# Float32 second products for block 1 of stage 1 and block 0 of stage 2, their weights split later, weight bits further ahead, idle products at the start

## The chip, the cores and the metric

One core of a Trainium2 chip runs the whole program. The metric is device microseconds of one execution; before the change the median of three runs is 1176.47 us (1175.05 to 1176.57). The core has five engines with their own in-order queues: PE (matrix products into PSUM; PEld is its weight load), DVE (elementwise), ACT (activation functions and copies), POOL (elementwise, and issue of its own DMAs) and SP, which here only issues DMAs.

## What is computed

Three things follow each other for 6080 tokens of 256 channels: a gated recurrence, a feed-forward with a rational activation, and a feed-forward with a squared relu. Both feed-forwards have 2048 hidden channels.

```python
f = lb + (1 - lb) * sigmoid(f_logit);  i = 1 - f
h[t] = f[t] * h[t-1] + i[t] * x[t]                  # over t; the recurrence's output is x1

h  = x1 @ w_in                                      # stage 1
P  = a0 + a1*h + a2*h**2 + a3*h**3
Q  = 1 + |b0|*|h| + |b1|*h**2
x2 = (P / (Q + 1e-6)) @ w_out

r  = maximum(x2 @ moe2_w_in, 0)                     # stage 2
out = (r * r) @ moe2_w_out
```

The weights arrive as 64-bit floats, two 32-bit words each.

## The kernel before

**Tiling.** The tokens are cut into 12 blocks (`BLOCKS`, one of 448, then eleven of 512). The hidden channels are cut into `NP` = 8 chunks of 256; a chunk's tile is 128 partitions x 2 x tokens. For block j and chunk i each stage does a first product into PSUM (`S1_mm1` into `h`, `S2_mm1` into `hb`), an elementwise chain, and a second product that adds to the block's accumulator over the eight chunks (`S1_mm2`, `S2_mm2` into `acc`). I call step s = 8j + i the turn in which chunk i of block j goes through stage 1. Stage 2 of the same block and chunk follows `LAG` = 9 steps later, so steps 0 to 7 are block 0 of stage 1 alone, steps 8 to 15 are block 1 (with block 0 of stage 2 from step 9 on), and so forth.

**Two kinds of product.** A product of float32 precision is made in one of two ways (`mm1`, `mm2`, lines 317 to 340). Either both operands stand as one float32 tile each, then there are 4 float32 matmuls to a group; or each operand stands as a high and a low part in the format fp32r, and three terms (high x high, low x high, high x low) are added, 12 matmuls that each run faster. In the trace one float32 matmul shows as two records. Block 0 of stage 1 is made with float32 products; all else with three terms.

**The chain of stage 1** (lines 381 to 445). ACT makes `u` = |h| (L387) and the linear part `s` (L394), from block 1 on POOL makes `t` from `u` (L389; in block 0 ACT squares h and PE adds the quadratic `q` with two diagonal matrices, L414). DVE makes the polynomial (L400, L401) and, from block 1 on, the quadratic (L408); ACT the reciprocal (L422, L423); DVE the ratio (L427, L430) and L441. The result goes to the second product as `g` in block 0 (L558), or as a high part on ACT (`s1_high`, L436) and a low part on DVE (`s1_low`, L444). In stage 2 ACT makes relu (L451), the square (L458) and the high part (L459), POOL the low part `g2l` one step later (`s2_low`, L464). When `acc` of a block is complete, ACT and DVE split it into `x2h` and `x2l` (L472, L473).

**Weights.** There are 32 chunks of weights, named by matrix and number: i1, o1 (stage 1, first and second product) and i2, o2. Each is loaded by SP (`load`), scaled by ACT (`scale`, L164), turned into float32 by three instructions on DVE (`bits`, L169, L178, L181, into a tile called `wa` or `whole`), and then split (`split_w`: two copies on ACT, L190 and L191, and one accumulating DMA from POOL's queue, L192). A float32 product uses the tile before its split.

**What sets the order.** The order is written out by hand, and each engine executes its own instructions in that order. One loop (lines 567 to 608) writes steps 0 to 7, a second (610 to 682) all the others. `h` has one buffer in PSUM (two in block 0), so the next first product waits until the polynomial has read it. In steps 8 to 16 the second loop makes bits and splits of i2 and o2 chunk by chunk, with these lines among others:

```python
wi = index["i2", s - NP] if s - NP < NP else None
wo = index["o2", s - LAG] if 0 <= s - LAG < NP else None
```

At the start the tokens of block 0 are turned by PE transposes (L225), gated and scanned; `first_gate`, `first_mul`, `pre_scan` come before the first `S1_mm1` (line 564), with the bits of chunk i1,0. The tokens of later blocks are prepared one block ahead (`ahead`: transposes, multiplications and scans on DVE, tanh on ACT, in steps 3 to 6 of a block).

## Time and profile before

| what | value |
|---|---|
| median of the runs | 1176.47 us |
| the profiled execution | 1175.87 us |
| its span, first to last instruction | 1174.1 us |
| PE busy | 1111.7 us (95%) |
| DVE busy | 986.9 us (84%) |
| ACT busy | 910.8 us (78%) |
| POOL busy | 416.3 us (35%) |

Busy shares over the whole span hide that the kernel has stretches with different limits. The span cut in 40 equal slices shows PE at 5 to 9 tenths in the first eight and at 9 in nearly all that follow, and DVE the other way at 9 in most of the first eight. The rows of a timeline give the start, the duration, the engine with its line, what is written and read with its shape, and in brackets how long the engine was idle before it and what ended that. Consecutive instructions of an engine overlap a little, so I take the distance from start to start as what one costs.

### The profile page before, as it was taken

To read this page: it belongs to the slowest core of one execution; us is meant where nothing else is said; L and a number is where in the kernel's file an instruction comes from. 1 tells how busy PE (TensorE), PEld (TensorE's weight loads), DVE (VectorE), ACT (ScalarE), POOL (GpSimd) and SP (SyncE) were. 2 spreads that over 40 slices of the span, in tenths; PEclk is the share of its full clock that TensorE was granted. 3 is DMA by queue.
4 is the path that set the end of the run, shared out by engine and by line. 5 is a ranking of instruction groups with operands and counts; after the bars stand their busy time and mean duration, and the time that the engine had idled before them with its cause. 6 is when DMAs were issued, how large, how long until landed. Compare 5 with 4: busy or idle time off the path is not lost.

```text
span 1174.1 us, 12592 instructions
## 1 busy us (share of the span) xinstructions
PE 1111.7 (95%) x4624; PEld 874.9 (75%) x4624; DVE 986.9 (84%) x949; ACT 910.8 (78%) x1052; POOL 416.3 (35%) x326
## 2 busy tenths in 40 slices
PE   5988778899999999999999999999999999999997
PEld 2445666688788788788788788788788788788876
DVE  4998989988888888988988988988988997997722
ACT  4877887788788778778778778778778778787754
POOL 1112343334334334334344333434434334333200
PEclk9999998999999999999999999999999999999999
DMA  9866222120020010010010010011010010000000
GB/s 239 276 160 122 49 54 36 28 52 1 1 48 7 1 36 19 1 36 19 1 36 18 1 37 18 1 36 19 1 36 19 1 36 19 1 19 1 1 18 18
DMA packets 85981, 44.66 MB, mean 38 GB/s; under 512 B 72736, under 2 KB 73632, under 8 KB 85920
## 3 DMA queue, kind: packets, MB, share of 16 engines
q1 hardware_dynamic: 80736, 35.01, 12.2%
q0 software_dynamic: 4704, 8.39, 4.3%
q8 instruction: 36, 0.59, 0.2%
q10 hardware_dynamic: 480, 0.46, 0.1%
q14 instruction: 25, 0.20, 0.1%
HBM read 29.23 MB, written 6.23 MB: 30 GB/s over the span
## 4 chain that ended last, share of the span: by engine, by line
PE 63%; POOL 8%; ACT 6%; DVE 4%; issue 4%; DMA 0%; DVEq 0%; ACTq 0%; POOLq 0%
PE acc L334 32%; PE h L323 16%; PE hb L323 15%; POOL g2l L464 4%; POOL t L389 3%; ACT u L387 2%; ACT g1h L436 1%; ACT g2h L459 1%; ACT L257 1%; ACT sg L257 1%; DVE t L427 1%; DVE s L430 1%; DVE s L401 1%; DVE s L400 1%; DVE whole L178 0%
## 5 line engine op out<-in xcount | busy, mean ns | idle before, releaser
L389 POOL TENSOR_SCALAR t<-u,pb 128x1024 f32<-128x1024 f32 x88 | 145.8, 1657 | 401.8 <-ACT u L387 401.8
L464 POOL TENSOR_TENSOR g2l<-r,g2h 128x1024 fp32r<-128x1024 f32 (+1 forms) x86 | 205.3, 2388 | 0.0
L323 PE MATMUL hb<-x2h,wi 128*128 128x512 f32 (+1 forms) x768 | 203.9, 387 | 0.2 <-ACT x2h L472 0.2
L334 PE MATMUL acc<-g2h,wo 128*128 128x512 f32 (+1 forms) x768 | 193.2, 392 | 0.7 <-ACT g2h L459 0.7
L408 DVE TENSOR_TENSOR t<-t,u 128x1024 f32<-128x1024 f32 x88 | 107.6, 1223 | 85.4 <-POOL t L389 85.2
L334 PEld LDWEIGHTS acc<-g2h,wo 128*128 128x128 f32 x768 | 148.2, 193 | 30.6 <-ACT g2h L459 2.0
L323 PEld LDWEIGHTS hb<-x2h,wi 128*128 128x128 f32 x768 | 144.1, 188 | 29.5 <-ACT x2h L472 0.6
L387 ACT ACTIVATE u<-h 128x1024 f32<-128x1024 f32 (+1 forms) x96 | 97.2, 1013 | 59.8 <-PE h L323 59.8
L422 ACT ACTIVATE u<-t 128x1024 f32<-128x1024 f32 x88 | 93.4, 1062 | 61.6 <-DVE t L408 61.5
L444 DVE TENSOR_TENSOR g1l<-t,g1h 128x1024 fp32r<-128x1024 f32 x88 | 119.0, 1353 | 20.9 <-ACT g1h L436 10.2
L334 PE MATMUL acc<-g2l,wo 128*128 128x512 f32 (+1 forms) x384 | 110.9, 410 | 23.4 <-POOL g2l L464 22.8
L436 ACT ACTIVATE g1h<-s 128x1024 fp32r<-128x1024 f32 x88 | 93.2, 1059 | 51.2 <-DVE s L430 49.9
L451 ACT ACTIVATE r<-hb 128x512 f32<-128x512 f32 (+1 forms) x192 | 109.7, 594 | 22.7 <-PE hb L323 16.8
L401 DVE SCALAR_TENSOR_TENSOR s<-s,pna,h 128x1024 f32<-128x1024 f32 (+1 forms) x96 | 121.9, 1270 | 3.4
L430 DVE SCALAR_TENSOR_TENSOR s<-s,pna,u 128x1024 f32<-128x1024 f32 (+1 forms) x96 | 121.2, 1263 | 0.0
L400 DVE TENSOR_TENSOR s<-s,h 128x1024 f32<-128x1024 f32 (+1 forms) x96 | 115.4, 1202 | 6.7 <-ACT s L394 6.7
L459 ACT ACTIVATE g2h<-r 128x1024 fp32r<-128x1024 f32 (+1 forms) x96 | 101.1, 1053 | 25.3 <-PE acc L334 20.2
L323 PE MATMUL hb<-x2l,wi 128*128 128x512 f32 (+1 forms) x384 | 117.6, 387 | 0.2 <-DVE x2l L473 0.2
L427 DVE SCALAR_TENSOR_TENSOR t<-t,u 128x1024 f32<-128x1024 f32 x88 | 114.8, 1304 | 2.9 <-ACT u L423 2.9
L394 ACT ACTIVATE s<-h,pna 128x1024 f32<-128x1024 f32 (+1 forms) x96 | 114.5, 1192 | 0.0
L323 PE MATMUL h<-x1h,wa 128*128 128x512 f32 x352 | 108.7, 401 | 6.1 <-DVE s L401 6.1
L334 PEld LDWEIGHTS acc<-g2l,wo 128*128 128x128 f32 x384 | 70.5, 195 | 54.4 <-POOL g2l L464 43.9
(104 smaller groups left out, 1838.9 us busy)
## 6 DMA issues: line engine op xcount, KB each, us to landing
wi<-in_moe_w_in_dram SPq DMA_DIRECT2D x12, 512.0 KB, 8.1
wo<-in_moe_w_out_dram SPq DMA_DIRECT2D x12, 512.0 KB, 4.6
z<-in_f_logit_dram SPq DMA_DIRECT2D x44, 128.0 KB, 3.4
x<-in_x_dram SPq DMA_DIRECT2D x44, 128.0 KB, 3.2
out_dram<-o SPq DMA_DIRECT2D x44, 128.0 KB, 2.9
wb<-wa POOLq DMA_DIRECT2D x14, 256.0 KB, 3.8
wi<-in_moe_w_out_dram SPq DMA_DIRECT2D x4, 512.0 KB, 8.7
wo<-in_moe_w_in_dram SPq DMA_DIRECT2D x4, 512.0 KB, 9.0
```

Of the source, the lines that this page charges most:

```text
L323: nc.tensor.matmul(out=o, lhsT=ws[a][:, k, fs], rhs=xs[b][:, k, :n], start=(q == 0 and k == 0), stop=(q == len(terms) - 1 and k == KD - 1),)
L334: nc.tensor.matmul(out=acc[:, dc, :n], lhsT=ws[a][:, c, dc::KD] if nm == "o2" else ws[a][:, c, dc * P:(dc + 1) * P], rhs=gs[b][:, c, :n], ...
L387: nc.scalar.activation(out=u, in_=h, func=ACTF.Abs)
L389: nc.gpsimd.tensor_scalar(out=t, in0=u, scalar1=pb[:, 1:2], scalar2=pb[:, 0:1], op0=ALU.mult, op1=ALU.add)
L394: nc.scalar.activation(out=s, in_=h, func=ACTF.Identity, scale=pna[:, 3:4], bias=pna[:, 2:3])
L400: nc.vector.tensor_tensor(out=s, in0=s, in1=h, op=ALU.mult)
L401: nc.vector.scalar_tensor_tensor(out=s, in0=s, scalar=pna[:, 1:2], in1=h, op0=ALU.add, op1=ALU.mult)
L427: nc.vector.scalar_tensor_tensor(out=o, in0=q, scalar=QC, in1=r, op0=ALU.add, op1=ALU.mult)
L430: nc.vector.scalar_tensor_tensor(out=s, in0=s, scalar=pna[:, 0:1], in1=u, op0=ALU.add, op1=ALU.mult)
L444: eng.tensor_tensor(out=fl, in0=t, in1=f32(fh), op=ALU.subtract)
L459: nc.scalar.activation(out=gh, in_=r, func=ACTF.Copy)
L464: eng.tensor_tensor(out=gl, in0=r, in1=f32(gh), op=ALU.subtract)
```

## The change

- **Second products in float32.** Block 1's second product of stage 1 takes one tile `g` (`s1_single`) and the float32 weights of o1; block 0's second product of stage 2 takes the squared relu itself and the float32 weights of o2. The high and low parts of both, `g1h`, `g1l`, `g2h`, `g2l`, are not made for these two blocks.
- **Splits.** o1 is split in steps 12 to 19, o2 in steps 10 to 17 (`do_splits`), each after its last float32 use; i1 in steps 0 to 7, i2 in steps 6 to 10. The places of the tiles in memory change with that (`whole_place`, `hi_lo`).
- **Bits further ahead.** Three chunks more than one are done before step 0's polynomial (i1,1, o1,0, i1,2; before, i1,1), two in each of the steps 0 to 10 and 15, one in each of the steps 11 to 14. The loads of i1,2 and o1,1 are issued ahead of the tokens `z` of block 1.
- **Order in block 1.** Steps 8 to 15 get a loop of their own. In it the linear activation stands ahead of |h|, the polynomial ahead of the quadratic, and `S1_mm1` of step 9 goes to PSUM's other buffer.
- **Idle products.** Six matmuls whose result nobody reads stand between the transposes of x and the first `S1_mm1`.

```diff
+        if nm == "o2":
+            if g % 2 == 0:
+                pairs[g // 2] = ch.tile(
+                    [P, 2, 512], I32, tag="g2l" if g // 2 % 2 else "g2h", name="whole"
+                )
+            return pairs[g // 2][:, g % 2, :]
...
-        other = j == 0 and i % 2 == 1
+        other = i % 2 == 1 and (j == 0 or (j, i) == (1, 1))
...
+        linear = dict(out=s, in_=h, func=ACTF.Identity, scale=pna[:, 3:4], bias=pna[:, 2:3])
+        if a[0] == 1:
+            nc.scalar.activation(**linear)
         nc.scalar.activation(out=u, in_=h, func=ACTF.Abs)
...
+    def s1_single(a, h, u, t, s):
+        g = ch.tile(
+            [P, 2, NMAX], F32, tag="g1l" if a[1] % 2 else "g1h", name="g"
+        )[:, :, :BLOCKS[a[0]]]
+        nc.vector.scalar_tensor_tensor(
+            out=g, in0=t, scalar=2.0, in1=s, op0=ALU.subtract, op1=ALU.mult
+        )
+        g1[a] = (g,)
...
     def s2_square(b, r):
+        nc.scalar.activation(out=r, in_=r, func=ACTF.Square)
+        if not b[0]:
+            g2[b] = (r,)
+            return None
         gh = chain_tile("g2h", F32R, BLOCKS[b[0]])
-        nc.scalar.activation(out=r, in_=r, func=ACTF.Square)
         nc.scalar.activation(out=gh, in_=r, func=ACTF.Copy)
...
         load(index["o1", 0])
+        load(index["i1", 2])
+        load(index["o1", 1])
         pre_load("z", zf, 1)
...
         xt = first_turn("x", ps_a, "acc2")
+        for _ in range(6):
+            nc.tensor.matmul(
+                out=ps_b.tile([P, NMAX], F32, tag="hb", name="warm")[:, :KD * P],
+                lhsT=diag[:, 1, :], rhs=raw[:, 0, :], start=True, stop=True,
+            )
         first_gate(zt)
...
+        slot_a = [("o1", g) for g in range(1, NP)] + [("i2", 2)]
+        slot_b = [("i1", g) for g in range(3, NP)] + [("i2", 0), ("i2", 1), ("i2", 3)]
...
+        second = {8: ("i2", 5), 15: ("o2", 7)} | {9 + g: ("o2", g) for g in range(6)}
...
+        def do_splits(s):
+            if 0 <= s - NP - 2 < NP:
+                split_w(index["o2", s - NP - 2])
+            if 0 <= s - NP - 4 < NP:
+                split_w(index["o1", s - NP - 4])
         S1_mm1(0, 0)
         c = s1_scalar((0, 0))
-        bits(index["i1", 1])
+        for of in (("i1", 1), ("o1", 0), ("i1", 2)):
+            bits(index[of])
...
+        for s in range(NP, 2 * NP):
+            i = s - NP
+            a, ap = (1, i), (1, i - 1) if i else (0, NP - 1)
+            b = (0, i - 1) if i else None
+            if i > 1:
+                S1_mm1(*a)
+            if i:
+                c = s1_scalar(a)
+            if s in first:
+                bits(index[first[s]])
+            do_loads(s)
+            s1_poly(*c)
+            q = s1_quad(a, *c)
+            if i == NP - 1:
+                split_x(2)
+            if b is not None:
+                S2_mm1(*b)
+                r = s2_relu(b)
+            for of in splits.get(s, ()):
+                split_w(index[of])
+            bits(index[second[s]])
+            S1_mm2(*ap)
+            if i == 0:
+                S1_mm1(1, 1)
+            s1_rsqrt(q, *c)
+            if i == 0:
+                to_x2(0)
+            s1_ratio(q, *c)
+            if i > 1:
+                S2_mm2(0, i - 2)
+            if b is not None:
+                s2_square(b, r)
+            do_splits(s)
+            ahead(a, ap)
+            s1_single(a, *c)
+            for t in (first, second):
+                if s + 1 in t:
+                    scale(index[t[s + 1]])
```

On DVE at the start, from the carry of block 0's scan to step 0's polynomial (`h_179` before, `h_192` after, is the first h; `wi_...` are raw weights), there stood before

```order
L300 COPY carry<-x_170 128x1 x2
L169 TENSOR_SCALAR wa_190<-wi_100 128x512
L178 SCALAR_TENSOR_TENSOR wa_190<-wi_100,wa_190 128x512
L181 SCALAR_TENSOR_TENSOR wa_190<-wi_100,wa_190 128x512
L400 TENSOR_TENSOR s<-s,h_179 128x2x448
L401 SCALAR_TENSOR_TENSOR s<-s,pna,h_179 128x2x448
```

and there stands now

```order
L302 COPY carry<-x_182 128x1 x2
L171 TENSOR_SCALAR wa_203<-wi_100 128x512
L180 SCALAR_TENSOR_TENSOR wa_203<-wi_100,wa_203 128x512
L183 SCALAR_TENSOR_TENSOR wa_203<-wi_100,wa_203 128x512
L171 TENSOR_SCALAR wb_207<-wi_102 128x512
L180 SCALAR_TENSOR_TENSOR wb_207<-wi_102,wb_207 128x512
L183 SCALAR_TENSOR_TENSOR wb_207<-wi_102,wb_207 128x512
L171 TENSOR_SCALAR wa_211<-wi_104 128x512
L180 SCALAR_TENSOR_TENSOR wa_211<-wi_104,wa_211 128x512
L183 SCALAR_TENSOR_TENSOR wa_211<-wi_104,wa_211 128x512
L405 TENSOR_TENSOR s<-s,h_192 128x2x448
```

so the bits of o1,0 (`wb_207`) and i1,2 (`wa_211`) moved ahead of the first polynomial.

On DVE in step 9 (`h_691` in both), after the polynomial's first instruction, up to the first one of step 10, there stood before

```order
L401 SCALAR_TENSOR_TENSOR s<-s,pna,h_691 128x1024
L169 TENSOR_SCALAR whole<-wo_648 128x512
L178 SCALAR_TENSOR_TENSOR whole<-wo_648,whole 128x512
L181 SCALAR_TENSOR_TENSOR whole<-wo_648,whole 128x512
L427 SCALAR_TENSOR_TENSOR t<-t,u 128x1024
L430 SCALAR_TENSOR_TENSOR s<-s,pna,u 128x1024
L441 SCALAR_TENSOR_TENSOR t<-t,s 128x1024
L444 TENSOR_TENSOR g1l<-t,g1h 128x1024
L169 TENSOR_SCALAR whole<-wi_515 128x512
L178 SCALAR_TENSOR_TENSOR whole<-wi_515,whole 128x512
L181 SCALAR_TENSOR_TENSOR whole<-wi_515,whole 128x512
L408 TENSOR_TENSOR t<-t,u 128x1024
```

and there stands now

```order
L406 SCALAR_TENSOR_TENSOR s<-s,pna,h_691 128x1024
L413 TENSOR_TENSOR t<-t,u 128x1024
L171 TENSOR_SCALAR whole<-wo_580 128x512
L180 SCALAR_TENSOR_TENSOR whole<-wo_580,whole 128x512
L183 SCALAR_TENSOR_TENSOR whole<-wo_580,whole 128x512
L442 SCALAR_TENSOR_TENSOR t<-t,u 128x1024
L445 SCALAR_TENSOR_TENSOR s<-s,pna,u 128x1024
L435 SCALAR_TENSOR_TENSOR g<-t,s 128x1024
L171 TENSOR_SCALAR wa_797<-wi_578 128x512
L180 SCALAR_TENSOR_TENSOR wa_797<-wi_578,wa_797 128x512
L183 SCALAR_TENSOR_TENSOR wa_797<-wi_578,wa_797 128x512
L405 TENSOR_TENSOR s<-s,h_778 128x1024
```

so g1l is gone, and the quadratic (L408, now L413) of each step moved behind its polynomial.

On PE in step 10, from the first product of stage 2 (`hb`) to the next first product of stage 1, there stood before

```order
L323 MATMUL hb<-x2l,wi_742 128x448 x2
L334 MATMUL acc_750<-g1h,wa_349 128x512 x4
L334 MATMUL acc_750<-g1h,wb_350 128x512 x4
L334 MATMUL acc_750<-g1l,wa_349 128x512 x4
L334 MATMUL acc_847<-g2h,wo_770 128x448 x8
L334 MATMUL acc_847<-g2l,wo_770 128x448 x4
L323 MATMUL h_883<-x1h,wa_460 128x512 x2
```

and there stands now

```order
L325 MATMUL hb<-x2l,wi_656 128x448 x2
L336 MATMUL acc_764<-g,wb_229 128x512 x4
L336 MATMUL acc_836<-r,whole 128x448 x4
L325 MATMUL h_854<-x1h,wc_426 128x512 x2
L325 MATMUL h_854<-x1h,wd_427 128x512 x2
```

so twenty-four matmuls of the two second products became eight float32 ones.

## Rows read from the trace of the kernel before

**Rows 1.** Busy time by stretch: us, then each engine's busy us, PEclk, DMA

```profile
24.24:106.20 81.96, 72.20 (x193) 35.38 (x191) 78.27 (x107) 66.49 (x99) 16.33 (x17) 1.00 0.76 202
106.20:220.55 114.35, 90.78 (x368) 74.02 (x367) 104.44 (x112) 92.00 (x124) 43.87 (x39) 0.93 0.28 48
...
236.07:1140.00 903.93, 896.52 (x3871) 727.66 (x3870) 773.50 (x695) 716.90 (x787) 345.63 (x252) 1.00 0.08 17
```

**Rows 2.** Timeline of PE: the first matmul of h in step 18

```profile
236.07 0.62 PE L323 MATMUL h<-x1h,wa 128*128 128x512 f32 x2
```

**Rows 3.** Timeline of DVE, step 9, from its polynomial to the next

```profile
119.84 1.21 DVE L400 TENSOR_TENSOR s<-s,h 128x1024 f32<-128x1024 f32 x1
...
122.29 0.42 DVE L169 TENSOR_SCALAR whole<-wo 128x512 int32<-128x512 uint32 x1
...
124.09 1.22 DVE L427 SCALAR_TENSOR_TENSOR t<-t,u 128x1024 f32<-128x1024 f32 x1
...
126.53 1.23 DVE L441 SCALAR_TENSOR_TENSOR t<-t,s 128x1024 f32<-128x1024 f32 x1
127.89 1.23 DVE L444 TENSOR_TENSOR g1l<-t,g1h 128x1024 fp32r<-128x1024 f32 x1
129.04 0.42 DVE L169 TENSOR_SCALAR whole<-wi 128x512 int32<-128x512 uint32 x1
...
131.78 1.21 DVE L408 TENSOR_TENSOR t<-t,u 128x1024 f32<-128x1024 f32 x1
132.92 1.21 DVE L400 TENSOR_TENSOR s<-s,h 128x1024 f32<-128x1024 f32 x1
```

**Rows 4.** Timeline of PE, from h of step 11 to h of step 12

```profile
136.29 0.62 PE L323 MATMUL h<-x1h,wa 128*128 128x512 f32 x2
...
139.01 0.97 PE L323 MATMUL hb<-x2h,wi 128*128 128x448 f32 x4
...
141.45 1.08 PE L334 MATMUL acc<-g1h,wa 128*128 128x512 f32 x4
...
144.18 1.79 PE L334 MATMUL acc<-g2h,wo 128*128 128x448 f32 x8
148.43 1.09 PE L334 MATMUL acc<-g2l,wo 128*128 128x448 f32 x4 [2.45 <-POOL g2l L464]
149.35 0.62 PE L323 MATMUL h<-x1h,wa 128*128 128x512 f32 x2
```

**Rows 5.** Timeline of PE: the first h, four float32 matmuls

```profile
15.74 5.72 PE L323 MATMUL h<-x,wa 128*128 128x448 f32 x8 [4.63 <-DVE carry L300]
```

**Rows 6.** Timeline of DVE: the first polynomial

```profile
24.24 1.09 DVE L400 TENSOR_TENSOR s<-s,h 128x896 f32<-128x896 f32 x1 [6.66 <-ACT s L394]
```

**Rows 7.** Timeline of PE: a second product of block 0, and what follows

```profile
45.73 3.17 PE L334 MATMUL acc<-g,wa 128*128 128x448 f32 x8
48.73 0.91 PE L414 MATMUL q<-u,diag 128*128 128x448 f32 x2
```

**Rows 8.** Timeline of ACT: scaling of the second and third chunk

```profile
12.00 0.67 ACT L164 ACTIVATE wi<-wi 128x512 f32<-128x512 f32 x1 [0.77 <-DMA wi<-in_moe_w_in_dram]
14.34 0.67 ACT L164 ACTIVATE wi<-wi 128x512 f32<-128x512 f32 x1 [1.67 <-DMA wi<-in_moe_w_out_dram]
```

**Rows 9.** Timeline of DVE: three waits, and a scan of block 2's tokens

```profile
94.75 1.29 DVE L311 TENSOR_TENSOR x1l<-sg,x1h 128x512 fp32r<-128x512 f32 x2 [1.54 <-ACT x1h L310]
...
109.30 1.09 DVE L473 TENSOR_TENSOR x2l<-acc,x2h 128x896 fp32r<-128x896 f32 x1 [0.57 <-ACT x2h L472]
...
166.49 0.43 DVE L169 TENSOR_SCALAR whole<-wo 128x512 int32<-128x512 uint32 x1 [3.13 <-DMA wi<-whole]
...
198.59 1.28 DVE L290 TENSOR_TENSOR_SCAN sg<-sg,carry,bx 128x512 f32<-128x512 f32 x1
```

**Rows 10.** Timeline of POOL in steps 9 and 10

```profile
129.79 1.54 POOL L389 TENSOR_SCALAR t<-u,pb 128x1024 f32<-128x1024 f32 x1 [3.19 <-ACT u L387]
...
133.21 2.10 POOL L464 TENSOR_TENSOR g2l<-r,g2h 128x896 fp32r<-128x896 f32 x1
```

130 lines of the change are left out of this document (51 added, 79 removed).

## The prediction

> **What bounds the kernel now.** I read the table of stretches first. It cuts the span where the schedule changes: into block 0 of stage 1 (steps 0 to 7), block 1 (steps 8 to 15) and the rest. In the rest PE is busy 896.5 of 903.9 us and DVE 773.5, so PE sets the pace. In the two stretches before it is the other way: DVE is busy 78.3 of 82.0 us and 104.4 of 114.4, PE 72.2 and 90.8 [rows 1]. So the first 236 us are a DVE schedule with a PE that waits, and from then on the time is PE work that this change doesn't touch. The question is therefore one number: how much earlier does PE reach step 18, whose first matmul h(2,2) starts at 236.07 [rows 2]? All after it moves along.
>
> Next I read one step of block 1 in DVE's order of time, step 9, from one L400 to the next: 119.84 to 132.92, 13.08 us without a gap [rows 3]. It holds the polynomial (L400, L401) 2.45, one chunk's bits 1.80, the ratio (L427, L430) 2.44, L441 1.36, the low part g1l 1.15, a second chunk's bits 2.74, and the quadratic (L408) 1.14; these are distances from start to start. Third, PE in step 11: h 2.72, hb 2.44, acc 2.73, then acc of stage 2 with a wait of 2.45 for POOL's g2l in its middle [rows 4]. Last, the start: the first h takes 5.72 us, while four float32 matmuls of the same 448 columns take 3.00 later [rows 5, 7], and DVE sits idle for 6.66 us behind it [rows 6].
>
> **The change, part by part.** I write poly(s) for the L400 of step s; it is 24.24 for step 0 and 106.20 for step 8, the bounds of the stretches in [rows 1].
>
> *Start.* Six idle float32 matmuls of 256 columns stand between the transposes of x, which end 4.63 before the first h at 11.1 [rows 5], and that h. At the speed of the first h (5.72 / 4 x 256 / 448 = 0.82 each) they last 4.9 us, to 16.0. The first h waits for the bits of its weights until 15.74 now, so it starts about 0.4 later. In the trace the four matmuls of that h, begun after 4.6 us of idleness, are slow by their duration, most of them at 1.2 GHz, and 3.00 is the time of four at 2.4 GHz [rows 5, 7]. If PE is kept busy until 16.1 the h should run in 3.1 and end at 19.2 instead of 21.46. ACT's three reads follow as now, and poly(0) comes 2.2 earlier: I take -2.1. Bounds: +0.4 if the clock doesn't rise in time (the idle matmuls then only delay), -2.7 if they are already quick.
> The chunks i1,2 and o1,0 now get their bits in DVE's idle time there. That is 2 x 1.80 = 3.6 of the 6.66 (less the 2.1), so it costs nothing if the weights are there. The ACT scale of the third chunk waited for its landing at 14.34 [rows 8]. The fourth chunk's load, now issued right behind it and ahead of z, should land about 2.3 later (the third came 2.3 behind the second, whose scale starts at 12.00): 16.7. That is before DVE wants it at 19.3. If it landed with the z packets ahead of it, ACT would stand on its scale, ahead of its reads of h; that is in the rivals.
>
> *Steps 0 to 7.* From poly(0) to poly(8) there are 15 chunks' bits now and 17 then: +3.6. The quadratic of step 8 goes behind poly(8): -1.14. The 1.54 that DVE waits for x1h [rows 9] should go, since h no longer waits for its own chunk's bits and ACT gets there sooner; if not, keep 1.5. Sum +0.9: 82.9 instead of 82.0, and poly(8) at 24.24 - 2.1 + 82.9 = 105.0. PE needs about 9 a step there (three groups of four float32 matmuls, 3.0 each [rows 7]), 73 in all against 82.9, so DVE stays the bound.
>
> *Steps 8 and 9.* Without g1l and with the quadratic after the polynomial a DVE step is 2.45 + 1.14 + 2.44 + 1.36 = 7.4 plus its bits. Poly(8) to poly(9) has two chunks, 3.6, and x2l, about 1.0, with a wait: x2h comes on ACT behind both rsqrt activations, which need the quadratic at 108.6, so it ends near 111.5 where DVE is ready at 110.4; now x2l waits 0.57 [rows 9]. I take 1.1 of wait: poly(9) at 105.0 + 13.1 = 118.1 (now 119.84). The product g(1,1) is done after 2.45 + 1.14 + 1.80 + 2.44 + 1.36 = 9.2, at 127.3.
>
> *From step 10 on, PE.* Here the work added counts. A float32 second product of four matmuls stands in place of twelve fp32r ones: for block 0 in stage 2 3.00 [rows 7] in place of 1.79 + 0.92 = 2.71 [rows 4]; for block 1 in stage 1, an estimate scaled from that row, 3.00 x 512 / 448 = 3.43 in place of 2.73 [rows 4]. Over sixteen products that is 8 x 0.29 + 8 x 0.70 = 7.9 us more PE work. It lies in a stretch in which PE has 23.6 us of idle time [rows 1], so it is paid only as far as PE becomes the bound, and I think it does: a PE step is 2.72 + 2.44 + 3.43 + 3.00 = 11.6, and nothing in it waits for POOL any more, because a float32 product needs no g2l. DVE needs 9.2, 10.4, 10.4, 10.4, 13.8 and 10.4 in steps 10 to 15 (7.4 plus bits, plus 1.2 each for the transposes, multiplications and x1l of block 2, pairs of 512 columns like the x1l of [rows 9], and 2.8 for its two scans of 1.28 with a copy each [rows 9]), together 64.6 against 69.5 for PE. ACT loses both fp32r copies, 16 of them; it is busy 92.0 of 114.4 now [rows 1], so it has room in steps of 11.6. Behind g(1,1) at 127.3 PE has 3.43 + 3.00 to h(1,3), at 133.7; six steps of 11.6 bring it to h(2,1) at 203.3; step 17, with one float32 product, is 2.72 + 2.72 + 2.73 + 3.00 = 11.2, so h(2,2) starts at 214.4 instead of 236.07: 21.7 earlier.
> Against that I set one low stretch of the clock. In steps 8 to 15 the granted clock averages 0.93 [rows 1], after PE's waits. PE still waits for x2 and for g(1,0) in steps 8 and 9. That is 0.07 x 114.4 / 0.5 = 16 us at 1.2 GHz. I keep a fifth of it, 3.4 us; it costs half, 1.7, if PE is late by it, and nothing if DVE is. Later splitting of o1 costs ACT 1.2 a step in steps 12 to 19, and is ready five steps before block 2 needs it; I cost it at nothing, and its bound is the 3.13 us that DVE stood for one such DMA in step 12 [rows 9].
>
> *Collisions of DVE and POOL.* Of the two chunks' bits in step 9 one takes 1.80 and the other 2.74 [rows 3]; beside the longer one, from 129.79, POOL runs its L389 [rows 10]. The polynomial reads one operand from PSUM; its L400 at 132.92 takes the same 1.21 as the one at 119.84 [rows 3] although POOL works on g2l from 133.21 [rows 10], so it isn't slowed. The change puts the linear activation ahead of u and the polynomial ahead of the quadratic, so L389 falls beside the polynomial. I take 0 for this. The Trainium skill, page "SBUF — State Buffer", section "Who interferes with whom", says that a DVE instruction with two SBUF inputs and a GpSimd one that reads SBUF block each other for a whole instruction, and that one with a single SBUF input doesn't; the rows agree. What it adds speaks against the change: where DVE runs late, u is early, L389 meets the ratio or the bits, and a whole L389 (1.54) would be lost in place of the 0.94 of the rows.
>
> **Sum.** The profiled execution took 1175.87, its span 1174.1. 1175.87 - 21.7 + 1.7 = 1155.9. The median of the runs is 0.6 above the profiled one: **1156.5**.
>
> **Rivals.**
> (a) *DVE stays the bound through block 1.* Its margin is 69.5 - 64.6 = 4.9 us in six steps. For: collisions as before, 0.94 in each of eight steps, 7.5; ACT's transposed tokens and their function that hold the next linear activation back by about 2 in step 11; a wait for ACT like the 0.57 and 1.54 of [rows 9] in half of the steps, 4. Less the margin that is 8.6: 1165. Against: the order of the instructions. By the page's rule, with a whole L389 in each step, the 7.5 would be 12.3 and the time 1170.
> (b) *The early bits come late*: the fourth chunk lands with z, that is behind the 0.5 MB of z and so another 2.3 to 7 us later than 16.7. At 23.3 ACT's reads of h start at 24 and poly(0) at 26.7 in place of 22.1: 1161. For: the queue is shared. Against: it is issued ahead of z.
> (c) *Better*: no low clock in steps 8 and 9 (1.7), idle matmuls quick at once (0.6), x2l without wait (1.1): 1153.
> (d) *It doesn't do what it says*: something of the new places of the weights (a chunk's slot still read by a DMA) holds a bits instruction in several steps by the 3.13 us seen once before [rows 9]; six of them give the gain back: 1174.
> (e) *Slower*: PE's clock. If PE waits over 2 us in every step from 10 to 17, as it does now [rows 4], the longer float32 groups run at 1.2 GHz. A PE step is then up to 23 instead of 11.6. It decides from the point where 40 us of these 93 are low (now 16 of 114): half of 40 is the gain of 20. With 60 us low it is 1186. For: the drops of before. Against: what ended the waits, POOL's g2l, is gone.
>
> **How the numbers follow.** Forecast 1156.5 with 0.58, (a) 0.20, (b) 0.07, (c) 0.07, (d) 0.03, (e) 0.05. The range 1151 to 1167 holds the forecast, (b), (c) and most of (a). What can be told from no change is 0.2%, 2.4 us: faster 0.92, same 0.03 (most of d), slower 0.05 (e).
>
> **What would show it.** First h at about 16.1 in 3.1 us; DVE's idle time before poly(0) under 3; poly(8) near 105; no g1l until step 16, no g2l until step 18; in steps 10 to 16 PE without waits and steps of 11.6; h(2,2) at 214 to 216; DVE busy about 95% in steps 10 to 15. Wrong if PE waits for g in several of these steps (a), if ACT waits for a weight DMA ahead of its first read of h (b), or if the granted clock is low in steps 10 to 16 (e).

## The result, and the profile after

The changed kernel takes 1161.18 us (1160.89 to 1162.4), the kernel before 1175.85 in the same session: ratio 0.9877, 95% interval 0.986 to 0.9895, that is 14.7 us less. The forecast was 1156.5, 19.4 less than the median it started from, in a range of 1151 to 1167. The profiled execution of the changed kernel took 1161.33, its span 1159.5, at a mean granted clock of 0.993.

I cut both spans at the same instructions: the polynomials of steps 0, 10 and 16, the first matmul of h(2,2), the end. The table of stretches for the changed kernel (us, then the busy time of PE, its weight loads, DVE, ACT, POOL, the granted clock, DMA share, GB/s):

```profile
22.22:132.02 109.80, 94.39 (x255) 50.20 (x254) 105.10 (x136) 82.63 (x120) 20.01 (x20) 0.94 0.61 161
132.02:205.09 73.07, 70.53 (x240) 45.09 (x239) 64.56 (x71) 54.64 (x76) 19.47 (x19) 1.00 0.28 47
```

and the same two stretches of the kernel before:

```profile
24.24:132.92 108.68, 92.83 (x270) 51.99 (x268) 102.16 (x130) 88.09 (x129) 23.39 (x24) 0.97 0.67 169
132.92:220.55 87.63, 70.16 (x291) 57.41 (x290) 80.55 (x88) 70.41 (x94) 36.82 (x32) 0.94 0.24 42
```

| stretch | before | after | change |
|---|---|---|---|
| start to poly(0) | 24.24 | 22.22 | -2.0 |
| poly(0) to poly(10) | 108.68 | 109.80 | +1.1 |
| poly(10) to poly(16) | 87.63 | 73.07 | -14.6 |
| poly(16) to h(2,2) | 15.52 | 15.19 | -0.3 |
| h(2,2) to the end of the span | 938.03 | 939.22 | +1.2 |

The other rows cancel, so the net gain lies in six steps, 10 to 15. There DVE had 80.6 us of work and has 64.6; POOL's went from 36.8 to 19.5, since g2l is gone. The second row hides a part of the gain: the changed kernel makes the bits of 21 chunks between poly(0) and poly(10), the kernel before those of 18, and three chunks are 5.4 us of DVE (1.80 each).

The start, in the timeline of PE (start, duration, engine, line, operation, out<-in, shapes, count, idle time ahead and who ended it), against [rows 5]:

```profile
11.28 5.16 PE L535 MATMUL warm<-x,diag 128*128 128x256 f32 x12
16.27 3.17 PE L325 MATMUL h<-x,wa 128*128 128x448 f32 x8
```

The idle matmuls end where h begins, and h takes 3.17 in place of 5.72. DVE's idle time ahead of poly(0), 6.66 in [rows 6], is down to 0.64:

```profile
22.22 1.09 DVE L405 TENSOR_TENSOR s<-s,h 128x896 f32<-128x896 f32 x1 [0.64 <-ACT s L401]
```

Steps 10 to 15, in the timeline of DVE, where the start of poly(12) to poly(14) is set by a wait for ACT:

```profile
155.16 1.22 DVE L405 TENSOR_TENSOR s<-s,h 128x1024 f32<-128x1024 f32 x1 [2.17 <-ACT u L393]
...
166.53 1.22 DVE L405 TENSOR_TENSOR s<-s,h 128x1024 f32<-128x1024 f32 x1 [0.74 <-ACT u L393]
...
172.41 1.22 DVE L442 SCALAR_TENSOR_TENSOR t<-t,u 128x1024 f32<-128x1024 f32 x1 [0.42 <-ACT u L428]
...
177.90 1.22 DVE L405 TENSOR_TENSOR s<-s,h 128x1024 f32<-128x1024 f32 x1 [0.73 <-ACT u L393]
...
192.61 1.21 DVE L405 TENSOR_TENSOR s<-s,h 128x1024 f32<-128x1024 f32 x1
...
205.09 1.21 DVE L405 TENSOR_TENSOR s<-s,h 128x1024 f32<-128x1024 f32 x1
```

and of PE, which waits for g in several of the same steps, where the wait for POOL's g2l in [rows 4] was:

```profile
165.84 3.70 PE L336 MATMUL acc<-g,wb 128*128 128x512 f32 x8 [0.71 <-DVE g L435]
...
190.16 3.70 PE L336 MATMUL acc<-g,wb 128*128 128x512 f32 x8 [0.79 <-DVE g L435]
...
202.91 3.70 PE L336 MATMUL acc<-g,whole 128*128 128x512 f32 x8 [0.85 <-DVE g L435]
...
220.28 0.97 PE L325 MATMUL h<-x1h,wc 128*128 128x512 f32 x2
```

The last row is h(2,2), at 220.28 instead of 236.07 [rows 2]; the forecast had 214.4. So DVE waits for ACT's u, and PE for DVE's g. None is the bound of the whole stretch: PE is busy 70.5 of its 73.1 us, DVE 64.6.

The round trip that DVE's waits belong to is a closed loop through ACT. In ACT's timeline, from one u to the next:

```profile
165.49 1.01 ACT L393 ACTIVATE u<-h 128x1024 f32<-128x1024 f32 x1
...
170.24 1.06 ACT L427 ACTIVATE u<-t 128x1024 f32<-128x1024 f32 x1 [2.87 <-DVE t L413]
171.32 1.06 ACT L428 ACTIVATE u<-u 128x1024 f32<-128x1024 f32 x1
172.29 0.94 ACT L472 ACTIVATE r<-r 128x896 f32<-128x896 f32 x1
173.13 0.62 ACT L192 ACTIVATE wo<-whole 128x512 fp32r<-128x512 f32 x1
...
175.21 0.67 ACT L166 ACTIVATE wo<-wo 128x512 f32<-128x512 f32 x1
175.78 1.19 ACT L392 ACTIVATE s<-h,pna 128x1024 f32<-128x1024 f32 x1
176.87 0.99 ACT L393 ACTIVATE u<-h 128x1024 f32<-128x1024 f32 x1
```

The polynomial starts when u ends (166.53, 177.90), the quadratic 2.45 behind it, the reciprocal root on ACT (L427) when the quadratic is done, and then ACT runs the root's square (L428), the square of relu (L472), four split copies (173.13 to 175.21), a scale, s and u, without a gap: 11.37 us a turn. Not every step is such a turn: from poly(11) to poly(12) it is 12.80, with ACT's function change in it (a table load of 1.28 at 150.12 and the tanh of block 2's tokens, 1.15), and from poly(14) to poly(15) 14.71, where DVE has its scans and two chunks' bits.

### The profile page after: what moved, and what is told of

It is laid out like the page before. It is cut to its first block, busy times and chain, and to the rows that moved or that the text cites. A ratio compares the mean times of both kernels' runs of the same rounds, so it can differ in the third digit from the quotient of the medians.

```text
span 1159.5 us, 12425 instructions
## 1 busy us (share of the span) xinstructions
PE 1118.4 (96%) x4572; PEld 863.8 (74%) x4572; DVE 974.8 (84%) x941; ACT 894.1 (77%) x1036; POOL 396.8 (34%) x310
## 4 chain that ended last, share of the span: by engine, by line
PE 69%; ACT 10%; DVE 8%; POOL 7%; issue 5%; DMA 1%; ACTq 0%; DVEq 0%; POOLq 0%
PE acc L336 34%; PE h L325 17%; PE hb L325 16%; POOL g2l L482 4%; POOL t L395 3%; ACT u L393 2%; DVE s L405 1%; ACT L259 1%; ACT g2h L477 1%; ACT sg L259 1%; DVE s L406 1%; DVE s L445 1%; DVE t L442 1%; DVE t L413 1%; ACT u L427 1%
## 5 line engine op out<-in xcount | busy, mean ns | idle before, releaser
L395 POOL TENSOR_SCALAR t<-u,pb 128x1024 f32<-128x1024 f32 x88 | 144.7, 1644 | 397.6 <-ACT u L393 390.1
L482 POOL TENSOR_TENSOR g2l<-r,g2h 128x1024 fp32r<-128x1024 f32 x78 | 188.7, 2419 | 0.0
L336 PE MATMUL acc<-g2h,wo 128*128 128x512 f32 x704 | 178.8, 395 | 0.7 <-ACT g2h L477 0.7
L413 DVE TENSOR_TENSOR t<-t,u 128x1024 f32<-128x1024 f32 x88 | 107.6, 1223 | 84.1 <-POOL t L395 84.0
L427 ACT ACTIVATE u<-t 128x1024 f32<-128x1024 f32 x88 | 93.5, 1062 | 84.2 <-DVE t L413 84.1
L336 PEld LDWEIGHTS acc<-g2h,wo 128*128 128x128 f32 x704 | 135.8, 193 | 29.5 <-ACT g2h L477 2.0
L459 DVE TENSOR_TENSOR g1l<-t,g1h 128x1024 fp32r<-128x1024 f32 x80 | 107.4, 1343 | 21.0 <-ACT g1h L451 11.9
L445 DVE SCALAR_TENSOR_TENSOR s<-s,pna,u 128x1024 f32<-128x1024 f32 (+1 forms) x96 | 122.0, 1271 | 0.0
L451 ACT ACTIVATE g1h<-s 128x1024 fp32r<-128x1024 f32 x80 | 84.7, 1058 | 39.8 <-DVE s L445 38.5
L325 PE MATMUL h<-x1h,wc 128*128 128x512 f32 x352 | 112.9, 402 | 0.0
L477 ACT ACTIVATE g2h<-r 128x1024 fp32r<-128x1024 f32 x88 | 93.4, 1062 | 24.1 <-PE acc L336 19.6
L325 PE MATMUL h<-x1l,wc 128*128 128x512 f32 x352 | 108.6, 390 | 0.0
L325 PE MATMUL h<-x1h,wd 128*128 128x512 f32 x352 | 108.6, 390 | 0.0
L336 PE MATMUL acc<-g2l,wo 128*128 128x512 f32 x352 | 101.0, 408 | 7.8 <-POOL g2l L482 7.1
```

Of the source, the lines that this page charges most:

```text
L325: nc.tensor.matmul(out=o, lhsT=ws[a][:, k, fs], rhs=xs[b][:, k, :n], start=(q == 0 and k == 0), stop=(q == len(terms) - 1 and k == KD - 1),)
L336: nc.tensor.matmul(out=acc[:, dc, :n], lhsT=ws[a][:, c, dc::KD] if nm == "o2" else ws[a][:, c, dc * P:(dc + 1) * P], rhs=gs[b][:, c, :n], ...
L395: nc.gpsimd.tensor_scalar(out=t, in0=u, scalar1=pb[:, 1:2], scalar2=pb[:, 0:1], op0=ALU.mult, op1=ALU.add)
L413: nc.vector.tensor_tensor(out=t, in0=t, in1=u, op=ALU.mult)
L445: nc.vector.scalar_tensor_tensor(out=s, in0=s, scalar=pna[:, 0:1], in1=u, op0=ALU.add, op1=ALU.mult)
L459: eng.tensor_tensor(out=fl, in0=t, in1=f32(fh), op=ALU.subtract)
```

## Experiments

The times are medians of four or five runs (eleven in one case), beside the kernel before. First where the gain comes from, then what bounds steps 10 to 15, then two attempts at more.

**The two float32 products, alone and together, in the kernel before.** Block 1's second product of stage 1 with one float32 factor (g1l and g1h go; the weights' high part serves as their float32 tile, and their low part is left out):

```
-                fh = s1_high(a, c[3])
-                s1_low(a, c[2], c[3], fh, nc.vector)
+                if a[0] == 1:
+                    g = ch.tile([P, 2, NMAX], F32, tag="g1l" if a[1] % 2 else "g1h", name="g")
+                    nc.vector.scalar_tensor_tensor(
+                        out=g, in0=c[2], scalar=2.0, in1=c[3], op0=ALU.subtract, op1=ALU.mult
+                    )
+                    g1[a] = (g,)
+                else: ...
```

> The kernel before with block 1's second product of stage 1 in float32, by four matmuls with the high part of the weights (their low part is left out in this block; the splits stay where they were). Theory (DVE is the bound in block 1): each of eight steps loses g1l, 1.15 us of DVE, and the copy g1h: 9.2 us less from step 8 to 15, with 5.6 us more PE work hidden: 1166.7. Rival (PE's waits for POOL's g2l and for h set the pace): 0 to -2, 1174 to 1176.

Measured 1164.48 (1163.89 to 1164.91), ratio 0.9902 (0.9887 to 0.9917): 11.3 less. More than the eight g1l of 1.15 on DVE (9.2). The rows give a likely source of the rest: before, it was 1.36 from the start of L441 to that of g1l [rows 3], and from g, which stands in L441's place, to the next start it is 1.14 in this run:

```profile
113.64 1.22 DVE L678 SCALAR_TENSOR_TENSOR g<-t,s 128x1024 f32<-128x1024 f32 x1
114.78 0.42 DVE L169 TENSOR_SCALAR whole<-wi 128x512 int32<-128x512 uint32 x1
```

Eight times 0.22 more makes 11.0. What ACT's eight copies g1h are worth beyond that was not separated.

Block 0's second product of stage 2 likewise, with the high part of its weights (g2l and g2h go):

```
         nc.scalar.activation(out=r, in_=r, func=ACTF.Square)
+        if not b[0]:
+            g2[b] = (r,)
+            return None
         gh = chain_tile("g2h", F32R, BLOCKS[b[0]])
```

> The kernel before with block 0's second product of stage 2 in float32, by four matmuls with the high part of the weights (their low part is left out in this block). It takes away POOL's g2l, the copy g2h on ACT and PE's 14.5 us of waits for g2l in steps 10 to 15, and nothing from DVE. Theory (DVE is the bound): the time moves by less than 2 us, 1174 to 1176. Rival (PE's waits for POOL are on the path): half of them or more come back, 1168 or less.

Measured 1173.97 (eleven runs), ratio 0.9985 (0.9976 to 0.9994): 1.8 less. The wait for g2l of 2.45 in [rows 4] was real, and yet its removal alone is worth little; before, DVE set the pace [rows 1].

Both:

> The kernel before with both of these products in float32 (high part of the weights alone in both). Theory: the sum of the two, 1165 to 1167; so of the 14.7 us that the whole change gives 9 to 10 come from the two products, 2.1 from the idle products, and about 3 from bits further ahead. Rival: with g1l gone PE's waits for POOL become the bound, then the two together give 2 to 4 us more than the sum of each alone.

Measured 1162.33 (1161.52 to 1164.28), ratio 0.9888 (0.9874 to 0.9901): 13.5 less, the sum of the two (13.1). So all but about one us of the change's 14.7 is there without bits further ahead, later splits, any new order or the idle products. What these runs leave out is the weights' low part; the later splits of the changed kernel are what keeps the full float32 weights for these products.

**The six idle products.** The changed kernel without them:

```
-        for _ in range(6):
-            nc.tensor.matmul(... name="warm" ...)
```

> The changed kernel without the six idle products (they change no result). Theory: the start is a chain from the first h through ACT to poly(0), and DVE sets the pace behind it. The first h takes 5.7 us again and ends at 21.5 instead of 19.4, poly(0) comes 2.1 later, at 24.3, and so does all that follows: 1163.3. Rival: PE's and DVE's waits in steps 8 and 9 take the delay up, and the time stays at 1161.2.

Measured 1163.07 (1162.48 to 1163.46), ratio 0.9894 (0.9879 to 0.9909): 1.9 more than the changed kernel. The first h on PE's timeline of this run:

```profile
15.04 6.10 PE L325 MATMUL h<-x,wa 128*128 128x448 f32 x8 [4.63 <-DVE carry L302]
```

It begins 1.2 earlier than in the changed kernel and ends 1.7 later; poly(0) comes at 23.93 in place of 22.22. The idle products pay by the speed of the four matmuls behind them.

**Both products and the idle products in the kernel before**, bits and splits left where they were:

> The kernel before with the two products in float32 and the six idle products at the start, and nothing else: weights are split, and bits made, where they were. Theory (bits further ahead, later splits and the new order bring nothing, and the three parts add up): 1162.3 - 1.9 = 1160.4, no slower than the changed kernel. Rival (the rest of the change is worth the 0.7 us by which the whole exceeds its parts, or needs the early start to pay): 1162 or more.

Measured 1161.14 (1160.39 to 1161.84), ratio 0.9878 (0.9865 to 0.9892): the time of the changed kernel. Here too the two products take the high part of the weights alone, so the later splits are bought for the result and not for time; the rest of the change as a whole brings no time. Its trace shows why. The same two stretches as above, poly(0) to poly(10) and poly(10) to poly(16), in this kernel:

```profile
22.58:127.60 105.02, 91.92 (x258) 48.55 (x257) 100.35 (x129) 85.49 (x126) 23.94 (x24) 0.98 0.72 178
127.60:205.07 77.47, 70.38 (x236) 44.80 (x235) 72.03 (x82) 58.61 (x82) 23.89 (x20) 0.98 0.27 48
```

By the groups of line 169 and 171 this kernel makes 18 chunks' bits in the first stretch and 11 in the second, the changed one 21 and 7. DVE is 96% busy in the first stretch in either, so what is moved into it is paid: 109.80 against 105.02, 4.8 more. In the second it gives back 77.47 - 73.07 = 4.4. Poly(16) starts at 205.07 here and at 205.09 there. PE still reaches h(2,2) later here, at 221.08 instead of 220.28; from there to the end it needs 938.5 in place of 939.2, and that evens it out.

**The order of s and u.** The changed kernel with u = |h| first again, ahead of the linear activation:

```
-        if a[0] == 1:
-            nc.scalar.activation(**linear)
         nc.scalar.activation(out=u, in_=h, func=ACTF.Abs)
```

> The changed kernel with |h| ahead of the linear activation in block 1, as before the change. Theory: the built program posts the completion of the two neighbours on ACT only once, behind the second, so the polynomial waits for both in either order; poly moves by 0.2 a step at most, and the time stays within 1 us of 1161.2. What changes is POOL: its L395 runs 1.0 earlier and may meet the bits. Rival (what the prediction took): the polynomial waits for the linear activation alone; then it starts 1.0 later in each step from 11 to 13 and the time is 3 to 5 us longer, 1165.

Measured 1161.4 (1160.56 to 1162.05), ratio 0.988 (0.9863 to 0.9896): the same. The polynomial needs s alone, but in the trace of the changed kernel poly(12) to poly(14) start when u ends, whose s had been done 0.9 earlier; here s is the later of the two, and poly(13) waits for s as long:

```profile
166.43 1.22 DVE L401 TENSOR_TENSOR s<-s,h 128x1024 f32<-128x1024 f32 x1 [0.74 <-ACT s L397]
```

In either order the polynomial starts when the second of the two ends, so putting s first frees nothing. That the built program signals the end of both only once, behind the second, is how I read this; the rows show the times alone.

**The split copies out of the loop.** The four copies a step later, and ahead of the reciprocal, where ACT waits 2.87 us for DVE:

```
                 r = s2_relu(b)
+            do_splits(s - 1)
...
-            do_splits(s)
...
```

> The changed kernel with the splits of steps 10 to 15 one step later and, in the step, ahead of the reciprocal, where ACT waits for the quadratic. Theory: in steps 11 to 15 a round trip is the bound, linear activation, |h|, polynomial, quadratic, reciprocal, its square, relu's square, the splits, scale, and the next linear activation: 11.4 us, of which the splits are 2.1. Without them it is 9.3, PE at 11.6 sets the pace, its five waits for g (3.2 in all) go, and h(2,2) starts at 217.5 instead of 220.3: 1158.5. Rival: DVE's own work is the bound, then poly(10) to poly(16) stays at 73.1 us and the time at 1161.2. Rival: the later splits hold the bits of o2,4 or o2,6, whose tiles they still read; then it is slower, 1163 to 1166.

Measured 1161.25 (1160.72 to 1161.97), ratio 0.9879 (0.9865 to 0.9894): no gain. The polynomials 12 to 14 in DVE's timeline, and ACT's linear activation ahead of each of the last two:

```profile
154.97 1.22 DVE L405 TENSOR_TENSOR s<-s,h 128x1024 f32<-128x1024 f32 x1 [2.16 <-ACT u L393]
...
165.53 1.21 DVE L405 TENSOR_TENSOR s<-s,h 128x1024 f32<-128x1024 f32 x1
...
177.29 1.22 DVE L405 TENSOR_TENSOR s<-s,h 128x1024 f32<-128x1024 f32 x1 [1.13 <-ACT u L393]
```

```profile
163.28 1.21 ACT L392 ACTIVATE s<-h,pna 128x1024 f32<-128x1024 f32 x1 [1.05 <-PE h L325]
...
175.13 1.21 ACT L392 ACTIVATE s<-h,pna 128x1024 f32<-128x1024 f32 x1 [2.36 <-PE h L325]
```

The turn of 11.37 fell to 10.56 once, in which ACT already waited 1.05 for PE's h; in the next it waited 2.36, and that turn took 11.76. The loop had been a bound, and PE's step, forecast at 11.6, stood right behind it: from h(1,3) to h(1,7) PE's steps are 11.6 to 11.9 here.

**Less work for PE.** Block 1's second product of stage 1 over one half of its 256 terms, four of the eight matmuls; the other half of the sum is left out:

```
-            for c in range(2):
+            for c in range(cs):            # cs = 1 for block 1 of stage 1
```

> The changed kernel with half of block 1's second product of stage 1: two float32 matmuls instead of four, 1.7 us less of PE in each of eight steps; half of that block's sum is left out. Theory (round trip of ACT and DVE is the bound in steps 10 to 15): poly(10) to poly(16) stays at 73 us, PE only waits longer for g, and what is gained is the last product's 1.7 behind g(1,7) and part of step 9's: 1158 to 1160. Rival (what the prediction took, PE is the bound): a PE step is 9.9 instead of 11.6 and h(2,2) comes 8 x 1.7 = 13.7 earlier: 1147.5.

Measured 1160.03 (1159.73 to 1160.33), ratio 0.9869 (0.9854 to 0.9883): 1.2 less, though PE lost 1.7 us in each of eight steps. The polynomials 12 to 14 and 16 here:

```profile
154.56 1.22 DVE L405 TENSOR_TENSOR s<-s,h 128x1024 f32<-128x1024 f32 x1 [2.15 <-ACT u L393]
165.93 1.22 DVE L405 TENSOR_TENSOR s<-s,h 128x1024 f32<-128x1024 f32 x1 [0.73 <-ACT u L393]
177.31 1.22 DVE L405 TENSOR_TENSOR s<-s,h 128x1024 f32<-128x1024 f32 x1 [0.74 <-ACT u L393]
...
204.53 1.21 DVE L405 TENSOR_TENSOR s<-s,h 128x1024 f32<-128x1024 f32 x1
```

The turns are 11.37 and 11.38 again, and from poly(10), at 131.45, to poly(16) it is 73.08 against 73.07. PE waits longer for g instead (2.60 in place of 0.71 in one step), and a part of what it saves goes into its clock, which is granted at 0.95 over that stretch in place of 1.00. The turns of 11.37 stay through all this, so PE's work alone does not set them.

**Less work for DVE.** The changed kernel without the last of the three bit instructions, for the chunks made in steps 8 to 15:

```
-        nc.vector.scalar_tensor_tensor(
-            out=e, in0=top, scalar=-(1 << 31), in1=e, op0=ALU.bitwise_and, op1=ALU.bitwise_or
-        )
```

> The changed kernel without the last of the three bit instructions (the one that puts the sign in, line 183) for the twelve chunks that are made in steps 8 to 15, so those weights lose their signs: 12 x 0.69 = 8.3 us of VectorE's work gone, eight of them (5.5 us) in steps 8 to 10 and 15, where VectorE does not wait, and four (2.8 us) in steps 11 to 14, where it waits 1.15 us a step for ScalarE's u already. Theory (VectorE's own work sets steps 8 to 10 and 15, its round trip with ScalarE sets steps 11 to 14): 1161.2 - 5.5 = 1155.7, of which TensorE's busy share in those steps may keep one or two: 1155 to 1158. Rival 1 (the round trip sets all of them): within 1 us of 1161.2. Rival 2 (VectorE sets all of them): 1152.9.

Measured 1157.02 (1156.45 to 1157.71), ratio 0.9844 (0.983 to 0.9857): 4.2 less, between the rivals, as expected. But where it came from was not. The polynomials 0, 10 and 16 of this run:

```profile
21.76 1.09 DVE L406 TENSOR_TENSOR s<-s,h 128x896 f32<-128x896 f32 x1 [0.42 <-ACT s L402]
...
128.14 1.21 DVE L406 TENSOR_TENSOR s<-s,h 128x1024 f32<-128x1024 f32 x1
...
200.67 1.21 DVE L406 TENSOR_TENSOR s<-s,h 128x1024 f32<-128x1024 f32 x1
```

From poly(0) to poly(10) five instructions of 0.69 are gone, 3.45 us, and the stretch is 106.38 in place of 109.80, 3.42 less. From poly(10) to poly(16) seven are gone, 4.8 us, and it is 72.53 in place of 73.07. Another 0.46 came before poly(0), where the edit changes nothing. What decides is not the stretch but the place in the step. Five of the seven stand behind the quadratics of steps 10 to 14, where DVE waits for ACT's second u anyway; that wait grows by what is taken out, in step 14 from 0.42 to 1.15. The sixth, in step 15, lengthens a wait for POOL's t further on from 1.10 to 1.63. The seventh stands in step 15 ahead of the polynomial, and from poly(14) to poly(15) it is 13.99 in place of 14.71:

```profile
174.35 1.22 DVE L406 TENSOR_TENSOR s<-s,h 128x1024 f32<-128x1024 f32 x1 [0.74 <-ACT u L394]
...
180.24 1.23 DVE L443 SCALAR_TENSOR_TENSOR t<-t,u 128x1024 f32<-128x1024 f32 x1 [1.15 <-ACT u L429]
...
188.34 1.21 DVE L406 TENSOR_TENSOR s<-s,h 128x1024 f32<-128x1024 f32 x1
```

Up to poly(10) it is the same: the two behind the quadratic went into waits for ACT (1.23 to 1.96, 0.43 to 1.16), the three ahead of polynomials brought the gain, with 1.3 us that DVE loses beside POOL in the changed kernel and not here. So 3.42 for 3.45 is chance, and DVE's work sets the time where it stands ahead of a polynomial that does not wait, in step 14 to 15 too.

**Both limits at once.** The same, with the split copies out of the loop:

> The same (twelve sign instructions left out) with the four split copies a step moved a step later and ahead of the reciprocal, which alone gave 1161.25. Theory (VectorE and, after it, its round trip set the steps): with VectorE's work shorter, the shorter round trip now counts too in steps 11 to 14 (some 0.7 a step), so 1 to 3 us less than the run with the signs alone left out. Rival (the copies' place never matters): within 0.7 us of that run.

Measured 1157.65 (1157.24 to 1158.51), ratio 0.985 (0.9836 to 0.9863): 0.6 more than the signs alone, so the theory fell and the rival held. With both eased PE goes from h(1,3) at 133.59 to h(2,2) at 215.52 in 81.9 us; the forecast for a PE without waits was 80.7, the changed kernel needs 84.5, and with the signs alone left out it is 82.3. With the signs alone left out PE is thus within 1.6 us of a PE that never waits, and the copies can free little more.

**A chunk moved.** One chunk's bits from step 15, ahead of its polynomial, to step 14, ahead of its polynomial:

```
-        first = {8: ("i2", 4), 9: ("i2", 6), 10: ("i2", 7), 15: ("o2", 6)}
+        first = {8: ("i2", 4), 9: ("i2", 6), 10: ("i2", 7), 14: ("o2", 6)}
```

> The changed kernel with one chunk's bits (o2, 6) made in step 14 ahead of the polynomial instead of step 15 ahead of it: 1.8 us of VectorE's work leaves the stretch from polynomial 14 to 15, where it did not wait (14.71 us), and comes into the one from 13 to 14, where it waited 1.15 us (11.37). Theory (VectorE's own work sets the first, the round trip the second): -1.8 + 0.7 = 1.1 less, 1160.1. Rival (only the sum of VectorE's work over the block counts): 1161.2. Rival (TensorE's products set both): 1161.2, with the waits for g unchanged.

Measured 1165.87 (1165.19 to 1166.97), ratio 0.992 (0.9906 to 0.9933): 4.7 slower, which no theory had. In DVE's timeline the bits wait for the DMA that still reads their tile, and the last of them is slow (POOL's L395 runs beside it from 179.34):

```profile
178.81 0.43 DVE L171 TENSOR_SCALAR whole<-wo 128x512 int32<-128x512 uint32 x1 [0.84 <-DMA wo<-whole]
...
180.09 1.49 DVE L183 SCALAR_TENSOR_TENSOR whole<-wo,whole 128x512 int32<-128x512 int32 x1
```

Poly(14) comes 14.2 behind poly(13) in place of 11.37, and g with it. PE waits for that g, and then:

```profile
193.75 6.30 PE L336 MATMUL acc<-g,wb 128*128 128x512 f32 x8 [3.59 <-DVE g L435]
```

```profile
193.75:199.89 6.14, 6.14 (x8) 2.57 (x9) 6.04 (x8) 3.51 (x6) 1.02 (x1) 0.57 0.02 3
```

Behind a wait of 3.59 the granted clock is 0.57 over the product, near the lower level of 1.2 GHz, and the product takes 6.30 in place of 3.70. The next h starts 18.09 behind the last one in place of 12.67: 2.8 of that is the longer wait, 2.6 the slower product. The polynomial of step 16 is late by it (15.77 behind the last, in place of 12.48). DVE's own time was only shifted from one step to the other (26.3 from poly(13) to poly(15) in place of 26.1); what it cost came through PE, by the later g and the clock behind it.

**The first bit instruction on GpSimd.**

```
-        nc.vector.tensor_scalar(
+        (engine or nc.vector).tensor_scalar(      # nc.gpsimd for the chunks of steps 8 to 15
```

> The changed kernel with the first of the three bit instructions (line 171, 0.42 us on VectorE) on GpSimd instead, for the twelve chunks made in steps 8 to 15: 5.0 us leave VectorE, 3.4 of them in steps 8 to 10 and 15, and GpSimd, busy 25.7 of the 99.2 us from polynomial 8 to 16, has the room. Leaving out the sign instructions (8.3 us, 5.5 in those steps) brought 4.2, so by the same ratio this brings 4.2 x 3.4 / 5.5 = 2.6: 1158.6. Rival (GpSimd beside VectorE on the same memory stretches VectorE's instructions, as its linear term does now, 2.10 for 1.22 us, or the bits come late): as much is given back, 1160.5 to 1163.

Measured 1168.2 (1167.47 to 1168.4), ratio 0.9935 (0.9922 to 0.9949): 7.0 slower than the changed kernel, worse than the rival too. On POOL the instruction takes 1.94 to 2.80 us, where DVE takes 0.42; the groups of DVE over steps 8 to 15 show the second bit instruction waiting for it (busy us and mean ns, then idle time ahead and who ended it):

```profile
L180 DVE SCALAR_TENSOR_TENSOR whole<-wo,whole 128x512 int32<-128x512 int32 x8 | 5.5, 690 | 6.8 <-POOL whole L171 6.8
L180 DVE SCALAR_TENSOR_TENSOR wa<-wi,wa 128x512 int32<-128x512 int32 x4 | 2.8, 691 | 7.6 <-POOL wa L171 7.6
```

14.4 us of waiting for 5.0 us saved. In steps 12 and 13, where the bits came in time, the run is a clean test: DVE has 0.42 less to do, its wait for ACT's second u grows from 0.42 to 0.88, and the polynomials stand at 159.68, 171.05 and 182.43, 11.37 and 11.38 apart as before. The bits stand behind the quadratic there, so what is taken from them goes into the wait; the loop sets those steps.

```profile
176.93 1.23 DVE L442 SCALAR_TENSOR_TENSOR t<-t,u 128x1024 f32<-128x1024 f32 x1 [0.88 <-ACT u L428]
```

## Why the prediction was right, and where it was off

The direction, the place and most of the size were right: DVE bounds the first 236 us, g1l's going frees it, and PE reaches h(2,2) earlier by that. It was some 5 us too much, and of the signs that the prediction named those for steps 10 to 15 did not come: PE does wait for g, which was its sign for rival (a), DVE is busy 88% and not 95%, and h(2,2) starts at 220.3, not by 216. Against the sum of the prediction (1155.9 for the profiled execution, measured 1161.33) the terms are:

*Start: right.* Forecast h at 16.1 in 3.1 and poly(0) at 22.1; measured 16.27 in 3.17, and 22.22. The run without the idle products shows the cause. Rival (b), the early bits late, did not come: DVE's only wait between the scan and poly(0) is 0.64, for ACT's s.

*Steps 0 to 7: nearly.* Forecast 82.9, measured 83.70 (105.92 - 22.22); the 0.8 is the first of the collisions below.

*Collisions at 0: wrong.* Two of DVE's instructions ran beside POOL's L395 between poly(7) and poly(9):

```profile
99.23 1.92 DVE L445 SCALAR_TENSOR_TENSOR s<-s,pna,u 128x896 f32<-128x896 f32 x1
...
116.06 2.10 DVE L435 SCALAR_TENSOR_TENSOR g<-t,s 128x1024 f32<-128x1024 f32 x1
```

```profile
99.03 1.19 POOL L395 TENSOR_SCALAR t<-u,pb 128x1024 f32<-128x1024 f32 x1 [5.54 <-ACT u L393]
...
115.82 1.28 POOL L395 TENSOR_SCALAR t<-u,pb 128x1024 f32<-128x1024 f32 x1 [7.41 <-ACT u L393]
```

They take 0.8 and 0.9 more than their kind does elsewhere (1.14 for L445 at 79.87, 1.22 for L435). The step that failed is "L389 falls beside the polynomial": in steps 8 and 9 u is ready when DVE is still in the step before. In steps 10 and 15 it is so again, and a bit instruction takes 1.41 (at 130.69) and 1.42 (at 190.54) in place of 0.69. In steps 11 to 14 L395 does fall beside the polynomial, which keeps its 1.22, as the prediction had it. So there were four collisions, 3.1 us in all, where rival (a) had eight. The Trainium skill, page "SBUF — State Buffer", section "Who interferes with whom", had it so: a DVE instruction with two SBUF inputs contends with a GpSimd one that reads SBUF. The rows agree. The prediction's warning from it, a whole L389 lost, holds as an upper bound: both times L395 had run 0.2 before DVE's instruction began, and 0.8 to 0.9 of its 1.2 to 1.3 was lost. Up to h(1,3) PE is 2.05 us late: 135.75, forecast 133.7. The first two collisions, 1.7, and a wait of 0.43 for ACT's second u ahead of the ratio of step 9 (125.83) are the bulk of it.

*Steps 10 to 15, "from step 10 on, PE": wrong, and the larger part.* The work was sized right, or nearly: DVE was forecast at 64.6 from poly(10) to poly(16) and has 64.56, partly by luck, since g takes 1.14 and not the 1.36 that the prediction kept from L441, and a collision adds 0.7; a PE step was forecast at 11.6, and PE is busy 70.5. The float32 product of 512 columns was estimated at 3.43; from start to start it is 3.54 behind a wait (169.38 - 165.84) and 3.44 without (181.02 - 177.58). What failed is the maximum of the two sums, 69.5 for PE against 64.6 for DVE. It left out the loop through ACT, 11.37 a turn, which stands just below PE's step of 11.6; and it took the maximum over the stretch, where the bound changes from step to step. The prediction's own list had DVE at 13.8 in step 14 beside a PE step of 11.6, and measured it is 14.71; ACT's function change makes 12.80 of step 11. From polynomial to polynomial the six steps are 10.34, 12.80, 11.37, 11.37, 14.71 and 12.48, and the short ones do not make up for the long. Halving one PE product gave nothing there, taking 4.8 us from DVE 0.5, shortening the loop 0.2 (131.36 to 204.19); easing DVE and loop together left PE 81.9, close to the forecast of 80.7. So h(1,3) to h(2,2) took 84.5, 3.8 more. Rival (a) named the pieces, the wait for ACT and its function change in step 11 (2.17 there, 0.74 in the steps behind it), and priced them at 8.6 for a DVE that stays the bound. The truth lies between it and the forecast. How the waits chain up step by step is argued from the rows; a run with the loop and PE both eased was not made.

*That the polynomial waits only for the linear activation* was an assumption of the change that I took over. It is wrong: the polynomial starts when the later of the two activations ends, and the run with the old order gives the same time.

*Low clock: mis-sized, and not paid.* Forecast 3.4 us at 1.2 GHz, costing 1.7. The granted clock is 0.50 for 10.3 us, behind a wait of 4.25 for x2h:

```profile
111.50:121.80 10.30, 8.34 (x16) 5.31 (x17) 8.98 (x9) 7.37 (x12) 2.40 (x3) 0.50 0.11 19
```

It cost nothing visible, as the prediction said for the case that DVE is late: further on PE still waits for DVE's g.

```profile
129.56 3.70 PE L336 MATMUL acc<-g,wb 128*128 128x512 f32 x8 [0.68 <-DVE g L435]
```

That the sum held 1.7 for it, which was not paid, is luck: without it the miss would have been 7.1. Of rival (e) nothing came: from poly(10) to poly(16) the granted clock is 1.00. Its condition, waits over 2 us in every step, was not in the kernel before either; there the one wait listed in step 14 is 1.76.

*After h(2,2)*: 939.2 in place of 938.0. The kernel with both products and idle products has 938.5 there, the run without the signs 939.2. Of the 1.2 there, 0.4 is in the first step, in which h(2,2) now begins behind a float32 product and its first matmul takes 0.97 in place of 0.62; the run with both products and idle products has that too. Most of the rest is in one step, from 242.61 to 254.79, which takes 12.18 in place of 11.33; in it PE waits 0.92 for POOL's g2l (at 253.73), and 0.24 in that run. What makes g2l late there stays open. Together: 2.05 + 3.8 - 1.7 + 1.2 = 5.4, which is 1161.3 - 1155.9.

*Bits further ahead: right for the place and incomplete.* The prediction costed the chunks where they go (+3.6), and where they leave only through the maximum that failed. Measured as a whole, +4.8 and -4.4. The gain stands without it.

A slip in the sums: rival (d)'s six waits of 3.13 make 1175, not 1174; it changes nothing.

## What to carry to other kernels

Where two engines' loads come within a tenth of each other, the maximum of their sums is not the time. Look for the closed loop that crosses engines (here poly, quadratic, reciprocal root, copies, s, u: 11.37) and put it beside them as a third candidate; if all three are close, expect that easing one gives almost nothing and price the change between the maximum and the rivals. Take the maximum step by step, since one long step is not made up by the others. And look where in the step an instruction stands: what was taken out ahead of a polynomial that did not wait counted, what was taken out in front of a wait only made the wait longer (0.42 to 1.15). Work moved to an earlier step is only gained if the step it goes to has slack: here both ends were nearly full, and four chunks' bits moved ahead brought 0.0. How few should be moved so that DVE's 8.5 us of idle time in steps 10 to 15 are used and the first stretch is not lengthened was not tried.
